# q's factors of units 10 and 11 contiguous, and another order of all engines, in a fused HGRN2 and leaky-ReLU MLP kernel

## The chip, the cores and the metric

One core of a Trainium2 chip runs the whole program. The metric is the device time of one execution in microseconds (us), as the median of several runs; a profile is taken of one further execution.

## The reference

A gated linear recurrence (HGRN2) over 768 steps feeds an MLP with a leaky ReLU. q, k, v and f_logit are [4, 8, 768, 48] (batch, heads, steps, head size), in float32.

```python
f = 1 / (1 + exp(-f_logit))
for t in range(S):
    state = f[:, :, t, :, None] * state + einsum('bhd,bhe->bhde', k[:, :, t], v[:, :, t])
    y[:, :, t] = einsum('bhd,bhde->bhe', q[:, :, t], state)
x = y.transpose(0, 2, 1, 3).reshape(3072, 384)
h = x @ w_in                      # w_in [384, 2048]
out = maximum(0.01 * h, h) @ w_out   # w_out [2048, 384]
```

## The kernel before

The recurrence is done in chunks of 128 steps, of which each batch has six. Work comes in twelve units `j`. Units 0 to 3 ("paired") hold one batch each, chunks 0 and 1 together. Units 4 to 11 ("unpaired") hold one chunk each of two batches: 4 and 5 are chunk 2 of batches 0, 1 and of 2, 3; 6 and 7 chunk 3; 8 and 9 chunk 4; 10 and 11 chunk 5, the last. `a` is 0 or 1 within a unit.

A unit runs so. Its f, k, q and v are loaded by SyncE's (SP's) queue (`Lf`, `Lk`, `Lq`, `Lv`, 192 KB each for one `a`, in pieces of 192 bytes for unpaired units). ScalarE (ACT) does the gate in two activations (`ge`, `gl`, lines L239 and L251); TensorE (PE) sums the log gates over steps (`cs`); ACT makes two sets of factors of the sums (`dec`), `em` for k (L306) and `at` for q (L308 or L311). VectorE (DVE) or GpSimd (POOL) multiply them into k and q (`k`, `q`, L322; L319 for the spread form). kh and qh are turned with the head size to the partitions: on PE for the paired units, and for the unpaired ones by two transposing DMAs in SP's queue (`xk`, `xq`, L363). PE then makes the scores (`sc`, L386), DVE masks them (`mk`, L400), PE mixes them with v and with the old state (`mx`, L417) and DVE or ACT copy the result to `xT` (`xt`). v is cast on DVE or POOL (`v`, L326). The state of a batch is carried on by `pt` (PE), `sf` (DVE) and `sb` (POOL, L510 and L513).

Then the MLP on PE: up-projections of 256 columns (`up`, L521) or, for the pairs of units 6, 7 and 8, 9, of 512 (`uw`, L532), the leaky ReLU on ACT (`pr`, L526, and `pv`, L535), and down-projections in four quarters (`dn`, L542; `dc`, L564, for half the columns of the last tile). `ob` copies a tile of the output from PSUM (L551, L553) to one of four buffers, and `st` stores it (L557). Weights are loaded (`WI`, `WO`) into the raw buffers of units 4 and 5 and cast (`ci`, `co`). `F` are matmuls on zeros whose results nobody reads.

`at` has two forms. Contiguous, it holds the 384 factors and behind them the factors at the chunk's end, which the state needs. Spread (`at_spread`), the factors stand so that two rows of 48 can be fetched by two small DMAs (`xe`, L295, 1.5 KB each) to a tile `end` on all the partitions that the state needs. Units 4 to 9 are in `SPREAD`; 10 and 11 have no state after them and need no `end`, but have the spread form too.

Every engine works in order and waits on semaphores. What stands in which place is written by hand in one string, `order`: each word is one operation of a unit, with the units and halves as numbers, the engine as a last number where there is a choice (0 DVE, 1 POOL or ACT, 2 both halves for loads of work that take a pair), and the PSUM banks behind `@`. The words are gone through from first to last, and each engine and SP's queue get theirs in that order; words of different engines beside each other say nothing of their times. Buffers are taken in turn: raw inputs by `j` mod 6, kh and qh by `j` mod 3, `at` by `j` mod 4, kT and qT by `j` mod 2, output buffers by `2j + a` mod 4.

Of the kernel before, what the change touches and what calls it, by code (L numbers as in the profile page):

```python
# [15 lines left out]
def kernel(  # L16
# [287 lines left out]
    def dec(j, a):  # L304
        t = banks[st[j]["cs", a]]
        nc.scalar.activation(ems[j % 2][:, a], t[:, 0:H * D], AF.Exp, scale=1.0)  # L306
        if spread(j):
            nc.scalar.activation(at_spread(j)[:, P2 * a:P2 * a + P2], t[:, 0:H * D].rearrange("t (p y d) -> t p y d", y=2, d=D),  # L308
                                 AF.Exp, scale=-1.0)
        else:  # L310
            nc.scalar.activation(at_of(j)[:, a], t[:, 0:H * D + P2], AF.Exp, scale=-1.0)  # L311
# [293 lines left out]
    tq_0_1@3 F_3_512@4 F_1_256@4 Lf_2_0 dec_1_1 k_1_1_1 tk_1_1@4 ge_2_1 gl_2_1 cs_2_1@2 Lq_1_0 WI_0 WI_1 sf_0_0
    sb_0_0 cq_0_1_1 ck_0_1_0 sc_0_1@5.7 F_1_512@3 F_1_256@3 ck_1_1_1 WI_5 q_1_1_1 tq_1_1@3 mk_0_0_0 sf_0_1
    Zk_2_0 mk_0_1_0 mk_0_0_1 Zb_1_0_1 sb_0_1 mk_0_1_1 WI_3 ge_1_0 gl_1_0 cs_1_0@0 v_1_1_1 cq_1_1_1 sc_1_1@6.4
    mk_1_1_1 mk_1_1_0 WI_2 dec_1_0 q_1_0_0 k_1_0_1 Lk_2_1 mx_0_2@5.1 ms_0 F_3_512@4 xt_0_1_0 dec_2_1 tq_1_0@3
    cq_1_0_0 ge_2_0 gl_2_0 Lq_2_1 xt_0_0_1 Lk_2_0 cs_2_0@7 dec_2_0 v_1_0_0 tk_1_0@0 F_2_512@3 F_1_256@3 ck_1_0_0
    sc_1_0@4.2 Lq_2_0 mk_1_0_1 Lv_2_1 pt_1_2@6.1 sf_1_0 ci_0_1 up_0_0@5 F_2_512@7 ci_1_1 up_0_1@3 ci_5_0  # L610
    up_0_5@0 mk_1_0_0 mx_1_2@7.2 xt_1_0_1 sb_1_0 sf_1_1 ms_1 Lv_2_0 ci_3_0 up_0_3@6 ci_2_0 up_0_2@4 xt_1_1_1
    up_1_2@1 up_1_1@7 k_2_1_1 tk_2_1@2 WI_4 WI_6 k_2_0_0 q_2_0_0 pr_0_0 up_1_5@5 pr_0_5 pr_0_2 ck_2_1_0 WO_0
    WO_1 pr_1_2 pr_0_1 q_2_1_1 tq_2_1@0 cq_2_1_0 tk_2_0@4 pr_1_5 Lf_3_1 WO_5 Lf_3_0 WO_3 ck_2_0_1 pr_0_3
    up_1_0@1 pr_1_0 tq_2_0@3 cq_2_0_0 v_2_0_0 up_1_3@2 pr_1_3 Mo WI_7 sc_2_0@5.0 mk_2_0_1 sc_2_1@4.6 mk_2_1_0
# [88 lines left out]
```

## Time and profile before

| | |
|---|---|
| median of 3 runs | 177.91 us (177.85 to 177.99) |
| the profiled execution's own time | 177.1 us |
| its span, from the first to the last instruction | 175.3 us |
| instructions | 5291 |
| HBM read and written | 25.17 MB and 4.72 MB, 170 GB/s over the span |
| granted TensorE clock | 1.000 |

A line of a group in the profile reads: source line, engine, operation, output<-input by the program's names, shape, count, then busy us and mean ns of one, then idle us of the engine just before. In a timeline, a row begins with start and length in us, and brackets at its end give the engine's idle time before it and what ended it. In a table by stretch, each row has the stretch, its length, then for PE, PE's weight loads, DVE, ACT and POOL the busy us and count, then the granted clock, the DMA share and GB/s. The DMA share is the busy share of the 16 DMA engines, and can pass 1 since packets overlap. SPq is SP's queue; its rows show how long the issue of a DMA held it.

### The profile page before, as it was taken

Reading aid. Unit: us, or ns where it says so; the run is one execution under the profiler, and the core shown is the slowest. Engines: PE = TensorE matmul, PEld = TensorE weight load, DVE = VectorE, ACT = ScalarE, POOL = GpSimd, SP = SyncE. Lnnn points to the kernel's source line nnn. Section 1 sums busy time; section 2 is a strip of 40 time slices with the busy share of each in tenths; the row PEclk is TensorE's granted clock in tenths of the full one; section 3 lists DMA queues with packets and bytes.
Section 4 is the critical chain, followed back from the end, with each engine's and each line's share of the span. In section 5 each row is a group of like instructions: output and inputs, shape, how many; then the busy total and the mean of one; then the engine's idle time right before and its main releaser. Section 6 shows DMA issues by size and latency. Waiting matters only on the chain.

```text
span 175.3 us, 5291 instructions
## 1 busy us (share of the span) xinstructions
PE 168.8 (96%) x2170; PEld 115.0 (66%) x2170; DVE 75.2 (43%) x159; ACT 110.2 (63%) x209; POOL 79.2 (45%) x131
## 2 busy tenths in 40 slices
...
DMA  5999988999995999999988899789989998411013
GB/s 155 323 313 354 287 232 271 384 265 293 228 227 126 224 196 233 148 191 196 175 172 193 184 175 222 163 163 188 226 171 237 187 209 174 105 40 45 0 59 124
DMA packets 109097, 34.45 MB, mean 197 GB/s; under 512 B 101776, under 2 KB 108048, under 8 KB 109072
## 3 DMA queue, kind: packets, MB, share of 16 engines
...
q8 instruction: 17, 0.28, 0.6%
...
HBM read 25.17 MB, written 4.72 MB: 170 GB/s over the span
## 4 chain that ended last, share of the span: by engine, by line
PE 45%; SPq 16%; DMA 11%; POOL 9%; DVE 8%; issue 5%; ACT 4%; POOLq 0%; DVEq 0%
PE ps L542 18%; PE ps L521 13%; SPq L212 9%; SPq L363 5%; PE ps L532 4%; DMA v_raw<-in_v_dram 4%; DMA k_raw<-in_k_dram 3%; DMA q_raw<-in_q_dram 2%; DMA out_dram<-osb 2%; PE ps L417 2%; DVE wm L400 2%; DVE wm L396 2%; SPq L295 2%; POOL kh L322 2%; PE ps L564 2%
## 5 line engine op out<-in xcount | busy, mean ns | idle before, releaser
L542 PE MATMUL ps<-w_out,gT 128*128 128x384 bf16 x368 | 66.6, 327 | 0.2 <-ACT gT L535 0.2
L542 PEld LDWEIGHTS <-gT 128*128 128x128 bf16 x368 | 34.9, 98 | 22.3 <-ACT gT L535 0.6
L526 ACT ACTIVATE gT<-ps 128x512 bf16<-128x512 f32 x64 | 34.8, 604 | 18.6 <-PE ps L521 18.2
L521 PE MATMUL ps<-xT,w_in 128*128 128x256 bf16 x384 | 45.6, 273 | 0.1
L521 PEld LDWEIGHTS <-w_in 128*128 128x128 bf16 x384 | 36.8, 98 | 6.4 <-DVE w_in L174 0.3
L400 DVE TENSOR_TENSOR wm<-ps,ut 128x512 bf16<-128x512 f32 x32 | 20.0, 684 | 25.3 <-PE ps L386 16.0
L322 POOL TENSOR_TENSOR kh<-k_raw,em 128x768 bf16<-128x768 f32 (+1 forms) x12 | 17.1, 1425 | 12.4 <-ACT em L306 5.9
L532 PE MATMUL ps<-xT,w_in 128*128 128x512 bf16 x96 | 22.1, 379 | 0.4 <-DVE osb L553 0.4
L535 ACT ACTIVATE gT<-ps 128x512 bf16<-128x512 f32 x32 | 17.7, 619 | 5.4 <-PE ps L532 5.1
L319 POOL TENSOR_TENSOR qh<-q_raw,at 128x768 bf16<-128x768 f32 x8 | 17.6, 2202 | 4.0 <-DMA q_raw<-in_q_dram 1.9
L513 POOL CAST sb<-sf 64x192 bf16<-64x192 f32 x40 | 14.9, 372 | 9.5 <-DVE sf L503 7.3
L553 DVE COPY osb<-ps 128x384 f32<-128x384 f32 x15 | 8.0, 553 | 24.2 <-PE ps L542 16.5
L306 ACT ACTIVATE em<-ps 128x384 bf16<-128x384 f32 x24 | 12.0, 500 | 8.8 <-PE ps L268 8.4
L475 ACT CAST xT<-ps 128x384 bf16<-128x384 f32 x15 | 7.2, 526 | 15.0 <-PE ps L417 15.0
L505 DVE TENSOR_TENSOR sf<-sf,ps 64x192 f32<-64x192 f32 x32 | 11.2, 350 | 12.3 <-PE ps L493 8.9
L532 PEld LDWEIGHTS <-w_in 128*128 128x128 bf16 x96 | 9.3, 98 | 10.9 <-issue 0.8
L510 POOL TENSOR_TENSOR sf<-sf,end 128x192 f32<-128x192 f32 x12 | 6.1, 506 | 20.8 <-DVE osb L553 11.0
L308 ACT ACTIVATE at<-ps 128x384 f32<-128x384 f32 x16 | 13.3, 831 | 0.0
L326 POOL CAST vb<-v_raw 128x384 bf16<-128x384 f32 (+1 forms) x9 | 6.1, 680 | 13.7 <-DMA v_raw<-in_v_dram 13.6
L239 ACT ACTIVATE f_raw<-f_raw 128x384 f32<-128x384 f32 (+1 forms) x16 | 11.0, 694 | 1.9 <-DMA f_raw<-in_f_logit_dram 1.9
L251 ACT ACTIVATE lf<-f_raw 128x384 bf16<-128x384 f32 (+1 forms) x16 | 11.0, 688 | 0.4
L396 DVE TENSOR_TENSOR wm<-ps,pair_mask 128x512 bf16<-128x512 f32 x16 | 10.4, 687 | 1.0 <-PE ps L379 0.8
...
## 6 DMA issues: line engine op xcount, KB each, us to landing
...
```

Of the source, the lines that this page charges most:

```text
L212: nc.sync.dma_start(out=raw(j, x)[:, a], in_=srcs[x][2 * h + a, :, c * C:(c + 1) * C, :].rearrange("h t d -> t h d"))
L308: nc.scalar.activation(at_spread(j)[:, P2 * a:P2 * a + P2], t[:, 0:H * D].rearrange("t (p y d) -> t p y d", y=2, d=D), AF.Exp, scale=-1.0)
L319: engine(e).tensor_mul(pairs(to[j % NR])[:, :, :, 0:D], pairs(raw(j, x)), at_spread(j))
L322: engine(e).tensor_mul(heads(j, to[j % NR], a)[:, :, :, 0:D], raw_heads(j, x, a), decays(j, by, a))
L396: nc.vector.tensor_mul(w.rearrange("t (s p) n -> t s p n", s=2), src.rearrange("t (s p n) -> t s p n", s=2, p=2), pair_mask[:, :, None, :] ...
L400: nc.vector.tensor_mul(w, src.rearrange("t (p n) -> t p n", p=P2), ut[:, None, :].to_broadcast([128, P2, 128]))
L513: nc.gpsimd.tensor_copy(out=sb[rows, :, y * D:y * D + D], in_=sf[rows])
L521: nc.tensor.matmul(pm[:, i, :], w_in_of(ff, kk), xT_of(j)[:, kk].rearrange("t a s -> t (a s)"), start=(kk == 0), stop=(kk == NK - 1))
L526: nc.scalar.activation(gT_of(j)[:, 2 * g:2 * g + 2, :], pm, AF.Prelu, alpha=0.01)
L532: nc.tensor.matmul(banks[bank], w_in_of(ff, kk), x[:, kk], start=(kk == 0), stop=(kk == NK - 1))
L535: nc.scalar.activation(gTs[n % 2][:, 512 * ff:512 * ff + 512], banks[st[2 * n].pop(("pw", ff))], AF.Prelu, alpha=0.01)
L542: nc.tensor.matmul(po, gT_of(j)[:, ff, 128 * a:128 * a + 128], w_out_b[ff // 2][:, ff % 2, :], start=(ff == 0), stop=(ff == NF - 1))
```

## The change

First, `spread(j)` is true for units 4 to 9 alone, so units 10 and 11 have the contiguous form, of 384 factors without those of the chunk's end. Their `q` product is then a plain product (L322) and no longer the spread one (L319).

Second, the whole `order` is another: the words are the same operations, but for the engine of some, the banks, one v load on ACT's queue in place of which a k load stands there now, and the zero matmuls, which are 22 of 512 and 4 of 256 columns before and 20 and 8 after.

```diff
     def spread(j):
-        return not paired(j) and (j in SPREAD or units[j][0] == NCH - 1)
+        return j in SPREAD
...
         else:
-            nc.scalar.activation(at_of(j)[:, a], t[:, 0:H * D + P2], AF.Exp, scale=-1.0)
+            n = H * D + P2 if paired(j) or chunk(j, a) < NCH - 1 else H * D
+            nc.scalar.activation(at_of(j)[:, a, 0:n], t[:, 0:n], AF.Exp, scale=-1.0)
...
     order = """
-    Zz Af_0_1 Av_0_0 F_9_512@7 Lf_0_0 Lf_1_1 Zl_1_1 Zk_0_0 Zb_2_0_1 Zv_2_1 Lk_0_0 Zv_0_0 Ms Lq_0_0 Mh Lv_0_1
+    Zz Af_0_1 Ak_0_1 F_9_512@7 Lf_0_0 Lk_0_0 Lf_1_1 Lq_0_0 Lq_0_1 Lv_0_1 Lv_0_0 Lf_1_0 Lk_1_1 Lq_1_1 Lv_1_1
...
```

Three places of the order. First SP's queue around the transposes of units 8 and 9 (kT0, qT0 are unit 8's, kT1, qT1 unit 9's; f_raw4 is f of unit 10, v_raw3 v of unit 9; `end` is written by the small transfers). Before:

```order
L212 DMA f_raw4_68<-in_f_logit_dram 128x8x48
L212 DMA q_raw3_79<-in_q_dram 128x8x48
L363 DMA_TRANSPOSE kT0_108<-kh2_93 128x8x128
L295 DMA end0_99<-at0_101 48x1x8
L363 DMA_TRANSPOSE qT0_110<-qh2_96 128x8x128
L295 DMA end1_100<-at1_102 48x1x8
L363 DMA_TRANSPOSE kT1_109<-kh0_91 128x8x128
L363 DMA_TRANSPOSE qT1_111<-qh0_94 128x8x128
L212 DMA v_raw3_85<-in_v_dram 128x8x48 x2
L295 DMA end1_100<-at1_102 48x1x8
L212 DMA f_raw5_69<-in_f_logit_dram 128x8x48
```

After:

```order
L558 DMA out_0_dram<-osb1_137 128x384
L364 DMA_TRANSPOSE kT0_108<-kh2_93 128x8x128
L364 DMA_TRANSPOSE qT0_110<-qh2_96 128x8x128
L558 DMA out_0_dram<-osb0_136 128x384
L364 DMA_TRANSPOSE kT1_109<-kh0_91 128x8x128
L364 DMA_TRANSPOSE qT1_111<-qh0_94 128x8x128
L212 DMA v_raw3_85<-in_v_dram 128x8x48 x2
L212 DMA f_raw4_68<-in_f_logit_dram 128x8x48
L212 DMA f_raw5_69<-in_f_logit_dram 128x8x48
L295 DMA end1_100<-at1_102 48x1x8
```

The two small transfers between the transposes are gone from there, a store stands in their place, and the second load of f for unit 10 moved from ahead of the four transposes to behind unit 9's v; 126 transfers of SP's queue stand ahead of it, where 117 did.

Second the same queue around the transposes of units 10 and 11 (kT0, qT0 and kT1, qT1; v_raw5 is v of unit 11). Before:

```order
L363 DMA_TRANSPOSE kT0_108<-kh1_92 128x8x128
L212 DMA k_raw5_75<-in_k_dram 128x8x48
L212 DMA q_raw5_81<-in_q_dram 128x8x48
L212 DMA k_raw5_75<-in_k_dram 128x8x48
L363 DMA_TRANSPOSE qT0_110<-qh1_95 128x8x128
L557 DMA out_0_dram<-osb0_136 128x384
L212 DMA v_raw5_87<-in_v_dram 128x8x48
L212 DMA v_raw4_86<-in_v_dram 128x8x48
L363 DMA_TRANSPOSE kT1_109<-kh2_93 128x8x128
L363 DMA_TRANSPOSE qT1_111<-qh2_96 128x8x128
L557 DMA out_0_dram<-osb1_137 128x384
L212 DMA v_raw5_87<-in_v_dram 128x8x48
```

After:

```order
L212 DMA k_raw5_75<-in_k_dram 128x8x48
L212 DMA v_raw4_86<-in_v_dram 128x8x48
L212 DMA q_raw5_81<-in_q_dram 128x8x48 x2
L212 DMA v_raw4_86<-in_v_dram 128x8x48
L558 DMA out_0_dram<-osb0_136 128x384
L364 DMA_TRANSPOSE kT0_108<-kh1_92 128x8x128
L364 DMA_TRANSPOSE qT0_110<-qh1_95 128x8x128
L558 DMA out_0_dram<-osb3_139 128x384
L364 DMA_TRANSPOSE kT1_109<-kh2_93 128x8x128
L364 DMA_TRANSPOSE qT1_111<-qh2_96 128x8x128
L558 DMA out_0_dram<-osb0_136 128x384
```

All loads now stand ahead of the four transposes, unit 11's second v among them.

Third, who makes kh and qh of units 10 and 11 (kh1, qh1 and kh2, qh2). Before, on POOL, its last rows:

```order
L322 TENSOR_TENSOR kh1_92<-k_raw4_74,em0_97 128x16x48
L319 TENSOR_TENSOR qh1_95<-q_raw4_80,at2_103 128x16x48
L510 TENSOR_TENSOR sf3_123<-sf3_123,end1_100 128x192
L513 CAST sb3_0_130<-sf3_123 64x4x48 x2
L510 TENSOR_TENSOR sf2_122<-sf2_122,end1_100 128x192
L513 CAST sb2_0_128<-sf2_122 64x4x48 x2
L510 TENSOR_TENSOR sf1_121<-sf1_121,end0_99 128x192
L513 CAST sb1_0_126<-sf1_121 64x4x48 x2
L322 TENSOR_TENSOR kh2_93<-k_raw5_75,em1_98 128x16x48
L319 TENSOR_TENSOR qh2_96<-q_raw5_81,at3_104 128x16x48
```

After, on DVE, for all but kh1, which stays on POOL:

```order
L323 TENSOR_TENSOR qh1_95<-q_raw4_80,at2_103 128x16x48
L554 COPY osb3_139<-ps6_146 128x384
L323 TENSOR_TENSOR kh2_93<-k_raw5_75,em1_98 128x16x48
L323 TENSOR_TENSOR qh2_96<-q_raw5_81,at3_104 128x16x48
L401 TENSOR_TENSOR wm1_113<-ps4_144,ut_154 128x512
```

The q products of units 5, 8 and 9 and the k products of units 6 and 9 went from POOL to DVE as well.

At other places that matter here: the first load of weights has 16 transfers of SP's queue ahead of it in both; the store for whose buffer the copy of unit 6's second tile waits stood behind unit 9's transposes and stands ahead of unit 8's; on ACT the gates of unit 10 stand ahead of the copy of unit 9's first half to `xT`; and the last up-projections of unit 11 before its first down chain are groups 2 and 3, which that chain's second quarter reads.

More of the change, by code (lines that the diff above doesn't have):

```diff
@@ L605 @@
[L605 to L614, printed above, removed]
@@ new lines @@
+    ck_1_1_1 cs_1_0@6 dec_1_0 q_1_0_0 tq_1_1@0 cq_1_1_1 mx_0_2@7.2 F_1_512@6 F_1_256@6 xt_0_0_0 Lq_2_1 WI_4
+    Lv_2_0 sb_0_0 ms_0 F_1_256@0 sf_0_1 tq_1_0@3 cq_1_0_0 Lv_2_1 v_1_1_1 sc_1_1@1.4 F_1_256@7 mk_1_1_0 mk_1_1_1
+    k_1_0_1 tk_1_0@6 v_1_0_1 ge_2_1 gl_2_1 cs_2_1@0 F_1_256@3 pt_1_2@7.5 sf_1_0 WI_6 ck_1_0_1 sc_1_0@3.6
+    F_1_512@1 mk_1_0_0 ci_0_1 WO_0 sb_1_0 ci_1_0 WO_1 ge_2_0 gl_2_0 cs_2_0@1 F_4_512@7 F_1_256@7 xt_0_1_1
+    up_0_0@4 F_1_512@3 pr_0_0 up_0_1@7 F_1_256@3 ci_5_0 up_0_5@2 sb_0_1 Lk_3_0 mk_1_0_1 mx_1_2@3.4 ms_1 Lf_3_0
@@ new lines @@
+    k_3_1_0 pr_0_7 dn_1_1_1 up_2_7@6 pr_2_7 dn_1_0_1 tk_3_1@2 co_5_0 Lk_5_0 Lk_5_1 dn_0_0_2 dn_1_0_2 dn_1_1_2
+    dn_0_1_2 dn_2_0_2 ck_3_1_1 ge_4_2 gl_4_2 cs_4_1@0 cs_4_0@6 dec_4_1 dec_4_0 xe_4_1 co_7_0 Lv_5_0 q_3_1_1
+    tq_3_1@2 co_6_1 Lq_5_0 Lq_5_1 dn_0_0_3 dn_1_1_3 dn_1_0_3 dn_0_1_3 ob_0_0_0 st_0_0 ob_1_1_1 st_1_1 ob_1_0_1
+    ob_0_1_1 st_0_1 cq_3_1_0 sc_3_1@0.3 v_4_2_1 sc_3_0@2.6 mk_3_0_1 mk_3_0_0 v_3_1_1 pt_3_2@1.7 dn_2_1_0@5
+    dn_2_1_1 dn_2_1_2 dn_2_1_3 sf_3_0 sb_3_0 ge_5_2 gl_5_2 cs_5_1@6 cs_5_0@2 dec_5_1 mk_3_1_0 mk_3_1_1
@@ new lines @@
+    mx_3_2@1.0 ms_3 xt_3_0_0 dn_2_0_3 k_4_2_1 xk_4 pt_4_0@3 pt_4_1@6 sf_4_0 sf_4_1 xt_3_1_1 up_3_5@1 up_3_4@0
+    up_3_2@3 up_3_0@6 pr_3_5 up_3_6@1 pr_3_4 up_3_3@0 dec_5_0 q_5_2_0 up_3_1@2 q_4_2_1 xq_4 pr_3_2 up_3_7@3
+    ob_2_0_0 pr_3_0 Lq_6_0 Lf_6_1 k_5_2_1 pr_3_1 dn_3_1_0@6 dn_3_0_0@4 pr_3_7 sf_3_1 sb_3_1 pr_3_3 dn_3_1_1
+    sc_4_2@2.7.3.0 mk_4_0_0 mk_4_1_0 mk_4_0_1 mk_4_1_1 dn_3_1_2 dn_3_0_1 dn_3_0_2 mx_4_2@2.3 xt_4_1_0 Lk_7_1
+    pr_3_6 dn_3_1_3 dn_3_0_3 Lf_6_0 ge_6_2 Lk_7_0 gl_6_2 cs_6_1@1 cs_6_0@7 dec_6_1 dec_6_0 Lv_5_1 xt_4_0_0
@@ new lines @@
+    dn_6_0_2 mx_8_2@1.7 xt_8_1_0 st_6_1 Lk_11_0 ge_10_2 gl_10_2 Lv_10_0 Lq_11_1 Lq_11_0 v_9_2_1 mx_9_2@3.2
+    xt_9_1_0 xt_9_0_1 Lv_10_1 dn_6_0_3 ob_6_0_1 st_6_0 sb_8_0 cs_10_0@0 dec_10_0 pt_9_1@5 sb_8_1 cs_10_1@7
+    dec_10_1 k_10_2_1 xk_10 pt_9_0@3 xt_8_0_0 uw_4_4@2 uw_4_13@1 uw_4_7@4 pv_4_7 uw_4_5@0 pv_4_5 uw_4_2@7 pv_4_2
+    uw_4_0@4 pv_4_0 uw_4_9@0 pv_4_9 pv_4_13 uw_4_8@7 pv_4_8 uw_4_14@4 uw_4_11@0 pv_4_11 uw_4_1@1 pv_4_14
+    uw_4_3@7 uw_4_15@0 uw_4_10@4 sf_9_0 uw_4_12@3 v_11_2_1 sf_9_1 uw_4_6@5 sb_9_1 pv_4_1 pv_4_3 dn_8_0_0@1
@@ new lines @@
+    dn_9_0_0@7 pv_4_4 dn_9_1_0@2 sb_9_0 q_10_2_0 xq_10 v_10_2_1 ob_7_1_0 dn_8_1_0@6 st_7_1 ge_11_2 gl_11_2
+    pv_4_12 cs_11_0@3 pv_4_6 cs_11_1@5 dn_8_0_1 dn_9_0_1 dn_8_1_1 dn_9_1_1 dec_11_1 pv_4_10 dn_9_0_2 dn_9_1_2
+    dn_8_0_2 dn_8_1_2 dec_11_0 k_11_2_0 xk_11 q_11_2_0 xq_11 pv_4_15 sc_10_2@5.4.3.0 mk_10_0_1 mk_10_1_0
+    mk_10_0_0 mk_10_1_1 dn_8_0_3 ob_8_0_1 dn_9_0_3 ob_9_0_0 dn_9_1_3 ob_9_1_1 mx_10_2@4.1 xt_10_0_0 xt_10_1_0
+    sc_11_2@3.5.0.2 mk_11_1_0 mk_11_0_0 mk_11_1_1 mk_11_0_1 dn_8_1_3 ob_8_1_0 up_10_0@7 up_10_1@4 pr_10_1
@@ L668 @@
+    dc_11_1_1_2 dc_11_1_0_0@4 dc_11_1_0_1 dc_11_1_1_3 oc_11_1_1_0 sh_11_1_1 dc_11_1_0_2 dc_11_1_0_3 oc_11_1_0_1
+    sh_11_1_0
     """
```

98 lines of the change are left out of this document (41 added, 57 removed).

## The prediction

> **What bounds the kernel now.** I read the page first (busy times, slices, chain), then busy time by stretch, then the timelines of PE, POOL and SP where the unpaired units run.
>
> ```profile
> PE 168.8 (96%) x2170; PEld 115.0 (66%) x2170; DVE 75.2 (43%) x159; ACT 110.2 (63%) x209; POOL 79.2 (45%) x131
> ...
> DMA  5999988999995999999988899789989998411013
> ...
> PE 45%; SPq 16%; DMA 11%; POOL 9%; DVE 8%; issue 5%; ACT 4%; POOLq 0%; DVEq 0%
> ```
>
> TensorE is busy for 96% of the span and looks like the only bound. But the 16 DMA engines are nearly as full until the 34th of the 40 slices, and the chain that ended last runs for 27% through SP's queue and through transfers. By stretch (the last two columns are DMA share and GB/s):
>
> ```profile
> 60.00:90.00 30.00, 30.00 (x361) 22.66 (x360) 10.70 (x22) 19.53 (x36) 15.40 (x14) 1.00 1.03 183
> 115.00:145.00 30.00, 29.04 (x305) 16.11 (x304) 10.10 (x20) 18.16 (x34) 15.30 (x19) 1.00 0.93 195
> ```
>
> So two queues run side by side, both full. At 195 GB/s one load of 192 KB takes 196,608 / 195e9 = 1.01 us. In the first stretch PE never waits; in the second it is idle for 0.96 us, in three waits of 0.17, 0.41 and 0.38:
>
> ```profile
> 117.23 1.15 PE L542 MATMUL ps<-w_out,gT 128*128 128x384 bf16 x6 [0.17 <-ACT gT L535]
> 121.56 0.62 PE L386 MATMUL ps<-qT,kT 48*128 48x128 bf16 x16 [0.41 <-DVE wm L400]
> ...
> 124.31 0.51 PE L417 MATMUL ps<-qT,sb 128*32 128x128 bf16 x24
> ...
> 129.81 4.05 PE L532 MATMUL ps<-xT,w_in 128*128 128x512 bf16 x18 [0.38 <-DVE osb L553]
> ...
> 148.99 0.62 PE L386 MATMUL ps<-qT,kT 48*128 48x128 bf16 x16
> ```
>
> ```profile
> 123.71 0.82 POOL L326 CAST vb<-v_raw 128x768 bf16<-128x768 f32 x1 [5.82 <-DMA v_raw<-in_v_dram]
> ...
> 143.58 2.19 POOL L319 TENSOR_TENSOR qh<-q_raw,at 128x768 bf16<-128x768 f32 x1
> ```
>
> POOL casts unit 9's v the moment it has landed, at 123.7 after 5.82 us of waiting, and PE mixes unit 9 at 124.31: the DMA queue sets PE's pace there. The last PE row is the scores of unit 11. What stands behind them on PE is the same set of operations in both kernels, so their start sets the end. SP's queue just ahead of such scores:
>
> ```profile
> 114.28 0.53 SPq L295 DMA_DIRECT2D end<-at  x1
> 114.91 1.25 SPq L363 DMA_TRANSPOSE qT<-qh  x1
> 116.26 0.53 SPq L295 DMA_DIRECT2D end<-at  x1
> 116.88 1.26 SPq L363 DMA_TRANSPOSE kT<-kh  x1
> 118.25 1.28 SPq L363 DMA_TRANSPOSE qT<-qh  x1
> ...
> 143.65 1.24 SPq L363 DMA_TRANSPOSE kT<-kh  x1
> 145.80 1.23 SPq L363 DMA_TRANSPOSE qT<-qh  x1
> ```
>
> ```profile
> qT<-qh SPq DMA_TRANSPOSE x8, 3.2
> ...
> end<-at SPq DMA_DIRECT2D x12, 1.5 KB, 2.4
> ```
>
> Unit 11's q transpose is issued at 145.80; with 3.2 us to landing that is 149.0, the start of the scores. POOL's product for it ends at 143.58 + 2.19 = 145.77, so SP stood from 144.89 to 145.80 for POOL: 0.91 us.
>
> **The change, part by part.**
>
> Zero matmuls. Before 22 of 512 columns and 4 of 256, after 20 and 8: two of 512 less and four of 256 more, the same columns. 0 us.
>
> q's factors of units 10 and 11. Four activations go from the spread to the contiguous form, whose nearest row is the paired units':
>
> ```profile
> L308 ACT ACTIVATE at<-ps 128x384 f32<-128x384 f32 x16 | 13.3, 831 | 0.0
> ...
> L311 ACT ACTIVATE at<-ps 128x388 f32<-128x388 f32 x8 | 4.1, 508 | 0.0
> ...
> L322 DVE TENSOR_TENSOR qh<-q_raw,at x5: 496/549/1205, 7.2 to 48.5; 128x384 bf16<-128x384 f32 x5
> ```
>
> 4 x (831 - 508) = 1.3 us of ACT. ACT is busy for 63% and PE waits for it 0.17 us in that stretch, so it counts 0; if this cover goes, the gain is up to 1.3.
>
> q's products. On POOL a spread one costs 2.2 us (the 2.19 above). After, those of units 5, 8, 9, 10 and 11 stand on DVE, and the k products of 6, 9 and 11 too. No row has such a DVE product of 768 columns: two of 384 at the median make 1.1 us, two of the longest 2.4. I take 1.1, for the median, with 2.4 for the range. Unit 11's two then take some 2.2 us on DVE, where POOL had to do state products first and took 1.6 + 2.2. SP's wait of 0.91 goes: -0.91. What is late next is the transfer queue itself.
>
> The end of SP's queue. Both v loads of unit 11 now stand ahead of the last four transposes; before, one of them stood behind. One load more ahead: +1.01.
>
> The small transfers of state factors (`end<-at`, 1.5 KB). Before, five of the twelve stand beside transposes or between them; after, one does, and the rest stand among loads and stores. The DMA share around these five, then around five that stand among loads (two of them in the window at 99.25):
>
> ```profile
> 75.50:76.50 1.00, 1.00 (x12) 0.90 (x10) 0.00 (x0) 1.00 (x3) 0.11 (x1) 1.00 0.25 35
> 83.75:84.25 0.50, 0.50 (x5) 0.29 (x4) 0.00 (x0) 0.50 (x2) 0.00 (x0) 1.00 0.45 83
> 92.50:93.50 1.00, 1.00 (x8) 0.61 (x7) 0.99 (x2) 1.00 (x2) 0.25 (x1) 1.00 0.23 41
> 115.50:116.25 0.75, 0.75 (x7) 0.43 (x6) 0.15 (x1) 0.72 (x2) 0.75 (x2) 1.00 0.22 38
> 117.50:118.25 0.75, 0.75 (x6) 0.29 (x4) 0.48 (x1) 0.00 (x0) 0.40 (x1) 1.00 0.20 36
> 96.25:97.25 1.00, 1.00 (x8) 0.61 (x7) 0.86 (x2) 0.00 (x0) 1.00 (x2) 1.00 0.29 66
> 99.25:99.75 0.50, 0.50 (x20) 0.46 (x12) 0.33 (x1) 0.50 (x3) 0.00 (x0) 1.00 0.46 114
> 123.00:123.50 0.50, 0.50 (x4) 0.14 (x2) 0.50 (x2) 0.00 (x0) 0.00 (x0) 1.00 0.43 59
> 129.25:130.00 0.75, 0.37 (x2) 0.10 (x1) 0.75 (x2) 0.54 (x1) 0.00 (x0) 1.00 0.26 46
> ```
>
> Lost time is the length times (1 - share). The first five: 0.75 + 0.28 + 0.77 + 0.59 + 0.60 = 2.99 us, 0.60 for each. The other four windows: 0.71 + 0.27 + 0.29 + 0.56 = 1.83, 0.37 for each of five transfers. Four that move save 4 x 0.23 = 0.9 us of the queue: -0.9, with bounds 0 (the transposes themselves make the holes) and -3.0 (all of the 2.99 goes). That some goes is likely from SP's rows: a transpose holds SP for 1.25 us, and the small transfer behind it for 0.53 more in which nothing large is issued.
>
> A rule of the Trainium skill speaks against this ("DMA: Bandwidth & Descriptors", Anatomy of one DMA): a transfer's fixed 2 us or so are mostly latency of completion and not setup, so a small one would hold nothing up behind it. The 2.4 us to landing of 1.5 KB agree with that figure. By the rule the moved transfers would save 0, and the sum would be 0.9 us higher.
>
> The queue's sum for unit 11's scores: 1.01 - 0.91 - 0.9 = -0.8 us.
>
> A second place, unit 10. Its second load of f stands behind unit 9's two v loads after, and stood ahead of unit 8's transposes before. Its gates on ACT:
>
> ```profile
> L239 ACT ACTIVATE f_raw<-f_raw 128x768 f32<-128x768 f32 x8 | 6.9, 861 | 0.0
> ...
> L251 ACT ACTIVATE lf<-f_raw 128x768 bf16<-128x768 f32 x8 | 6.8, 854 | 0.2
> ...
> 148.17 0.89 PE ps L417 x56
> ...
> 163.79 1.30 PE ps L542 x8
> ```
>
> It lands one load behind 123.7, at 124.7, less 0.9 at 123.8; with 0.86 + 0.85 and 0.1 of hand-over PE has its sums to do at 125.6. At the pace of before PE stands there at 124.31 + 0.89 for the mix + 0.65 for four down matmuls = 125.85. So PE may be 0.25 ahead there, and the 0.38 at 129.81 goes too, since unit 6's copy, for which it waits, hung on a store that is now issued ahead of unit 8's transposes: -0.6. Between -0.6 and -0.8 I take -0.7. The waits of 0.17 and 0.41 stand ahead of where the queue binds, so their going adds nothing.
>
> The start. PE's first up-projection stands at 18.55, and POOL casts its weights as they land:
>
> ```profile
> 16.33 0.82 POOL L174 CAST w_in<-f_raw 128x768 bf16<-128x768 f32 x1 [0.85 <-DMA f_raw<-in_moe_w_in_dram]
> ...
> 18.55 0.83 PE L521 MATMUL ps<-xT,w_in 128*128 128x256 bf16 x6
> ```
>
> As many transfers stand ahead of these weights after as before, so it comes up to 1.4 us earlier (18.55 - 17.15). I count 0, because PE gives back what it gains where the queue binds later. Bounds -1.4 and +0.5 (POOL's first products stand behind more clearing).
>
> The tail. The last two up groups of unit 11 now feed the second quarter of its first down chain, with one group of four down matmuls between them and it:
>
> ```profile
> L526 ACT ACTIVATE gT<-ps 128x512 bf16<-128x512 f32 x64 | 34.8, 604 | 18.6 <-PE ps L521 18.2
> ```
>
> Four down matmuls cover 0.65 us; the activation needs 0.60 and its two hand-overs some 0.2 to 0.3 (an estimate from the 0.17 above): +0.2, bounds 0 and 0.4.
>
> **Sum.** -0.7 + 0.2 = -0.5 us. The profiled execution took 177.1 us (a span of 175.3 and 1.8 around it), so 176.6. The median of the runs, 177.91, stands 0.8 above it: the forecast is 177.4.
>
> **Rivals.** 0.2% is 0.36 us, which I take for what can be told from no change.
>
> First, the queue gives nothing back, since the holes belong to the transposes, which remain. Then 1.01 - 0.91 + 0.2 = +0.3: 178.2, no change to be told. For it: the same bytes go through engines at a share of 0.93 to 1.03. Against it: the holes at 115.5 and 117.5, each beside a small transfer, are the deepest of all. By the page's rule above this is the outcome.
>
> Second, slower, by the late load of f for unit 10. PE stands at unit 10's sums for ACT's gates, and on ACT the copy that the wide up-projection of units 8 and 9 needs is queued behind them. It decides if that load lands after 124.0 (125.85 - 1.8). With no saving it lands at 124.7 and PE goes on at 126.5, 0.65 late; with 0.38 given back and 0.2 of tail that is +0.5, 178.4, and if one more load's time is lost in the queue, 179.4. For it: nine more transfers stand ahead of it than before. Against it: 0.7 us of saving is enough.
>
> Third, much faster: the 2.99 us of holes go, and the start keeps its gain. Then PE alone binds, its 0.96 us of waits end, and -1.4 - 0.96 + 0.2 = -2.2 gives 175.7. Against it: the queue would have to be ahead everywhere.
>
> **How the numbers follow.** The forecast has 0.45 and the third 0.1, both faster: 0.55. The first has 0.2: same. The second has 0.25: slower. The forecast's own range is 176.5 to 177.7 (a saving of 0.6 to 1.8); with the rivals' ends 175.9 to 178.5 leaves out 2 in 10.
>
> **What would show it.** Right: unit 11's scores start near 148.3; SP waits for no product ahead of the last q transpose; PE has no wait for `osb` in the wide up-projection of units 8 and 9; the DMA share between the transposes of units 8 and 9 is over 0.5. Wrong: PE idle ended by ACT's `lf` (L251) near 125 (the second rival); unit 11's scores at 149 or later with the transposes back to back (the first); DVE products of 768 columns at 2 us or more beside POOL's, which would put the 0.91 back.

## The result, and the profile after

The changed kernel took 178.81 us (median; 177.42 to 180.78) beside 177.81 us for the kernel before: a ratio of 1.0055, with a 95% interval of 1.003 to 1.008. It ran twice more, in other comparisons: 177.49 beside 177.59 us (1.0021, 0.9994 to 1.0049) and 177.39 beside 177.62 us (1.0014, 0.9988 to 1.004). So the change makes nothing faster; it costs nothing that can be told, or about half a per cent. The forecast of 177.4 us stood for a ratio of 0.997; that the repeats' times lie beside 177.4 is luck, since the kernel before took 177.6 there and not 177.91. The ratios count fast runs alone and are not the quotients of the medians, which are 0.9994 and 0.9987 in the repeats.

The time has two parts, the span from the first to the last instruction and what lies around it. In the repeats the median span is 175.4 and 175.2 us beside 175.8 for the kernel before, so 0.4 and 0.6 shorter (the means are 0.1 and 0.2 shorter). What lies around it is 2.08 to 2.26 us in all 44 runs of the changed kernel and 1.73 to 1.86 in all the runs of the kernel before that stand beside the experiments: medians of 2.12 to 2.15 and of 1.78. So what the repeats win inside the span, some 0.35 us outside it takes back.

The first execution profiled took 179.84 us, 1.0 above its median, with a span of 177.6 us. A second and a third took spans of 175.4 and 174.9. I show the first, and then what of it stood again. The busy line, the DMA share and the chain of its page:

```profile
PE 168.9 (95%) x2169; PEld 114.9 (65%) x2172; DVE 86.8 (49%) x170; ACT 110.8 (62%) x206; POOL 70.6 (40%) x123
...
DMA  5999999998994999996999988968896999120202
...
PE 59%; DMA 12%; POOL 8%; SPq 8%; issue 5%; DVE 4%; ACT 3%; POOLq 0%; ACTq 0%
```

TensorE's work is the same 169 us; DVE has 11.6 us more and POOL 8.6 less, as the products moved. PE's timeline, the rows with idle time in brackets and unit 11's scores:

```profile
91.94 0.62 PE L387 MATMUL ps<-qT,kT 48*128 48x128 bf16 x16 [0.62 <-ACT gT L527]
...
116.55 0.81 PE L533 MATMUL ps<-xT,w_in 128*128 128x512 bf16 x3 [0.90 <-DVE sf L506]
117.94 2.11 PE L543 MATMUL ps<-w_out,gT 128*128 128x384 bf16 x12 [0.58 <-DVE sf L506]
...
123.65 0.62 PE L387 MATMUL ps<-qT,kT 48*128 48x128 bf16 x16 [0.34 <-DMA qT<-qh]
...
151.22 0.62 PE L387 MATMUL ps<-qT,kT 48*128 48x128 bf16 x16
```

The waits of 0.41 and 0.38 that I had read before 130 us are replaced by others. The longest, 0.90, is for DVE's state sums of unit 8 (`sf`, L506), which free the PSUM bank of the next wide up-projection; 0.58 for the second of these sums follows at once. POOL, DVE and SP in that place:

```profile
113.74 1.57 POOL L511 TENSOR_TENSOR sf<-sf,end 128x192 f32<-128x192 f32 x1 [1.50 <-DMA end<-at]
```

```profile
113.46 1.47 DVE L320 TENSOR_TENSOR qh<-q_raw,at 128x768 bf16<-128x768 f32 x1 [3.69 <-DMA q_raw<-in_q_dram]
115.74 0.76 DVE L506 TENSOR_TENSOR sf<-sf,ps 64x192 f32<-64x192 f32 x2 [0.81 <-POOL sb L514]
117.13 0.76 DVE L506 TENSOR_TENSOR sf<-sf,ps 64x192 f32<-64x192 f32 x2 [0.63 <-POOL sb L514]
117.92 0.96 DVE L323 TENSOR_TENSOR kh<-k_raw,em 128x768 bf16<-128x768 f32 x1
118.80 1.45 DVE L320 TENSOR_TENSOR qh<-q_raw,at 128x768 bf16<-128x768 f32 x1
```

```profile
110.00 0.77 SPq L295 DMA_DIRECT2D end<-at  x1
...
115.00 1.23 SPq L364 DMA_TRANSPOSE qT<-qh  x1
116.28 0.57 SPq L558 DMA_DIRECT2D out_dram<-osb  x1
118.91 1.24 SPq L364 DMA_TRANSPOSE kT<-kh  x1
120.31 1.25 SPq L364 DMA_TRANSPOSE qT<-qh  x1
```

Read from the bottom up, this is a chain through four engines. SP has nothing to do from 116.85 to 118.91 (2.05 us): it waits for unit 9's k product on DVE. That product starts only at 117.92, behind two pairs of state sums. These wait for POOL's state products of unit 6, and the first of those waits until 113.74 for a transfer of 1.5 KB that SP issued at 110.00. Before, the last of unit 9's transposes was issued at 118.25; here at 120.31.

I call this the state chain. The second profile has it too, without the wait for the transfer:

```profile
111.59 1.61 POOL L511 TENSOR_TENSOR sf<-sf,end 128x192 f32<-128x192 f32 x1
...
113.64 0.76 DVE L506 TENSOR_TENSOR sf<-sf,ps 64x192 f32<-64x192 f32 x2 [0.81 <-POOL sb L514]
...
113.26 1.43 SPq L364 DMA_TRANSPOSE qT<-qh  x1
114.74 0.57 SPq L558 DMA_DIRECT2D out_dram<-osb  x1
116.81 1.24 SPq L364 DMA_TRANSPOSE kT<-kh  x1
118.22 1.25 SPq L364 DMA_TRANSPOSE qT<-qh  x1
```

Here unit 8's q transpose is issued 1.65 us earlier than before (113.26 for 114.91), so the order does gain on the queue there; then SP waits 1.50 us for unit 9's k product, and the last transpose is issued at 118.22, where it was before (118.25). The gain is spent in one wait. In the third profile these are 112.49, a wait of 1.97, and 117.81; in the first, where unit 8's q transpose went out at 115.00, there was no gain to spend.

### The profile page after: what moved, and what is told of

Its sections match the earlier page's. It is cut to its first block, busy times and chain, and to the rows that moved or that the text cites. A ratio compares the mean times of both kernels' runs of the same rounds, so it can differ in the third digit from the quotient of the medians.

```text
span 177.6 us, 5295 instructions
## 1 busy us (share of the span) xinstructions
PE 168.9 (95%) x2169; PEld 114.9 (65%) x2172; DVE 86.8 (49%) x170; ACT 110.8 (62%) x206; POOL 70.6 (40%) x123
## 4 chain that ended last, share of the span: by engine, by line
PE 59%; DMA 12%; POOL 8%; SPq 8%; issue 5%; DVE 4%; ACT 3%; POOLq 0%; ACTq 0%
PE ps L543 22%; PE ps L522 18%; SPq L212 5%; PE ps L418 4%; DMA v_raw<-in_v_dram 4%; DMA qT<-qh 4%; PE ps L533 4%; POOL qh L320 2%; DMA end<-at 2%; POOL sf L511 2%; POOL sb L514 2%; DMA f_raw<-in_f_logit_dram 2%; PE ps L387 2%; SPq L558 2%; PE ps L565 1%
## 5 line engine op out<-in xcount | busy, mean ns | idle before, releaser
L543 PE MATMUL ps<-w_out,gT 128*128 128x384 bf16 x368 | 65.3, 326 | 0.7 <-DVE sf L506 0.6
L527 ACT ACTIVATE gT<-ps 128x512 bf16<-128x512 f32 x64 | 36.1, 605 | 19.1 <-PE ps L522 14.7
L536 ACT ACTIVATE gT<-ps 128x512 bf16<-128x512 f32 x32 | 18.1, 604 | 5.0 <-PE ps L533 4.4
L514 POOL CAST sb<-sf 64x192 bf16<-64x192 f32 x40 | 16.3, 408 | 11.9 <-DVE sf L504 9.4
L327 POOL CAST vb<-v_raw 128x768 bf16<-128x768 f32 (+1 forms) x13 | 9.5, 738 | 18.7 <-DMA v_raw<-in_v_dram 18.4
L554 DVE COPY osb<-ps 128x384 f32<-128x384 f32 x12 | 6.6, 553 | 20.4 <-PE ps L543 10.9
L511 POOL TENSOR_TENSOR sf<-sf,end 128x192 f32<-128x192 f32 x12 | 7.1, 593 | 21.0 <-DVE osb L554 10.5
L323 POOL TENSOR_TENSOR kh<-k_raw,em 128x768 bf16<-128x768 f32 (+1 forms) x9 | 11.9, 1318 | 8.5 <-ACT gT L536 5.5
L552 ACT COPY osb<-ps 128x384 f32<-128x384 f32 x11 | 5.1, 491 | 13.3 <-PE ps L543 13.2
L506 DVE TENSOR_TENSOR sf<-sf,ps 64x192 f32<-64x192 f32 x32 | 11.2, 350 | 3.8 <-POOL sb L514 1.4
L323 DVE TENSOR_TENSOR kh<-k_raw,em 128x384 bf16<-128x384 f32 (+1 forms) x7 | 5.6, 807 | 11.0 <-ACT em L306 10.9
L100 PE MATMUL ps<-zeros 128*128 128x512 bf16 (+1 forms) x28 | 9.3, 430 | 1.2 <-DVE zeros L93 1.1
```

Source lines behind the costliest of these rows:

```text
L323: engine(e).tensor_mul(heads(j, to[j % NR], a)[:, :, :, 0:D], raw_heads(j, x, a), decays(j, by, a))
L506: nc.vector.tensor_add(sf[rows], sf[rows], new)
L514: nc.gpsimd.tensor_copy(out=sb[rows, :, y * D:y * D + D], in_=sf[rows])
L527: nc.scalar.activation(gT_of(j)[:, 2 * g:2 * g + 2, :], pm, AF.Prelu, alpha=0.01)
L536: nc.scalar.activation(gTs[n % 2][:, 512 * ff:512 * ff + 512], banks[st[2 * n].pop(("pw", ff))], AF.Prelu, alpha=0.01)
L543: nc.tensor.matmul(po, gT_of(j)[:, ff, 128 * a:128 * a + 128], w_out_b[ff // 2][:, ff % 2, :], start=(ff == 0), stop=(ff == NF - 1))
```

## The experiments

The theory: the order gains on the transfer queue, and SP gives it back in waits for products that stand on DVE behind work that is itself late (unit 9's behind the state sums, unit 6's k product behind two state sums and a copy). The rivals: the transfers set the pace whatever their order; or the loss lies in the opening, in the layout, or in the last units. In each, the ratio is to the kernel before on the same chip. In the cuts of the order, a plus marks a word put in and a minus one taken out.

**after_again.** No edit.

> The changed kernel once more, beside the others of this call. Its first profile was of an execution of 179.84 us, 1.0 above the median of 178.81, so that its waits may overstate what the change costs. Theory of the state chain (the 0.90 us that TensorE waits near 116.5 for DVE's state sums of unit 8, and SP's wait of 2.05 us for unit 9's k product behind them, belong to the order): both waits stand in this profile again, within 0.5 us. Rival (they were chance of one execution: a small transfer that happened to take 3.7 us to land): they are gone or under 0.3 us, at the same median of 178.8. A third place, the wait of 0.62 us ahead of unit 6's scores, is asked in the same way.

177.49 us, 1.0021 (0.9994 to 1.0049). The 0.62 at 92 us was gone, the 0.90 and 0.58 shrank to one wait of 0.29, and SP's wait to 1.50:

```profile
115.85 2.11 PE L543 MATMUL ps<-w_out,gT 128*128 128x384 bf16 x12 [0.29 <-DVE sf L506]
...
121.58 0.62 PE L387 MATMUL ps<-qT,kT 48*128 48x128 bf16 x16 [0.36 <-DMA qT<-qh]
```

This is between the two expectations. SP's wait for unit 9's k product belongs to the order: it stood in all three profiles, and with it a wait of 0.34 to 0.36 of TensorE for unit 9's q transpose. TensorE's waits for the state sums do not stand: they fell under 0.3 here, which was the rival's mark, and were gone in the third profile. The half per cent of the first comparison does not come back.

**end_early.** Three small transfers earlier, in one row.

```
  xe_7_0 +xe_7_1 +xe_6_1 +xe_6_0 Lf_9_1 Lv_8_1 Lq_9_0 Lk_8_0 ...
  ... -xe_7_1 sb_7_1 sb_7_0 Lq_9_1 -xe_6_1 ... q_8_2_0 -xe_6_0 sb_6_0 sf_8_0 sb_6_1 sf_8_1
```

> The changed kernel, with three small transfers of state factors (both halves of unit 6, the second of unit 7) moved up SP's queue to stand behind the first of unit 7, near 97.9 us, in place of 106.1, 107.3 and 110.0. No other queue changes. Theory of the state chain: POOL then has its state products of units 6 and 7 done by about 109, DVE's state sums of unit 8 wait for no one, TensorE's 0.90 us near 116.5 and SP's 2.05 us go, unit 9's scores start some 1 to 2 us earlier against the work ahead of them: about 177.8, 1.0 below the changed kernel. Rival (the whole transfer queue is late, and the next load takes the place of what goes): 178.6 to 178.9. Second rival (three more small transfers ahead of the loads cost the 0.4 to 0.6 us each that I had read from the holes in the DMA share): unit 8's products are 1 to 2 us later, 178.8 to 179.5.

177.31 us, 0.9986 (0.9963 to 1.0008); the changed kernel itself took 177.49 beside it, so the 1.0 us expected did not come. SP's wait for unit 9's k product was gone (0.17 us), yet unit 9's q transpose was issued at 118.25 again. The row of four small transfers took its price ahead of it:

```profile
96.00:98.00 2.00, 2.00 (x53) 1.41 (x54) 2.00 (x5) 1.10 (x3) 0.94 (x2) 1.00 0.93 230
98.00:100.00 2.00, 2.00 (x97) 1.64 (x86) 1.62 (x5) 1.48 (x3) 0.07 (x1) 1.00 0.08 11
100.00:102.00 2.00, 1.95 (x16) 1.10 (x16) 1.84 (x6) 0.20 (x1) 0.00 (x0) 1.00 0.72 137
```

By stretch, with the DMA share next to last: SP issued the four from 96.18 to 98.63, and for two microseconds the DMA engines then had almost nothing. That is 1.84 + 0.56 = 2.4 us of the queue. Without the row, in the second profile of the changed kernel, the last two stretches had shares of 0.93 and 0.77, so the three transfers that moved cost 1.70 + 0.10 = 1.8 us more, 0.6 for each.

**before_opening.** The kernel before up to about 21 us, the changed order behind.

```
  the first 158 steps of the order before, then the changed order's steps without those done
```

> The order of the kernel before up to about 21 us (the first 158 steps), and from there the changed kernel's order without the steps already done (six steps differ, two PSUM banks are renamed). The layout is the changed one. In the profiles TensorE's first up-projection stood at 18.55 before and at 19.19 after. Theory of the opening (0.64 us are lost there, and TensorE is too full afterwards to win them back): about 178.2, 0.6 below the changed kernel. Rival (what is lost there would be spent again in waits for the transfer queue at 92 and at 116): 178.7 to 178.9, with longer waits at these places.

178.12 us, 1.005 (1.0026 to 1.0075). TensorE's first up-projection stood at 18.50, but unit 2's mix at 32.20 (32.15 in the changed kernel, 32.00 before): all but 0.15 of the 0.64 us of the opening are given back within 14 us. So the opening is not where the time goes. That the time is near the 178.2 expected is luck: it is above the 177.49 of the changed kernel beside it, and was to be below. The state chain stood, with an SP wait of 2.03 and 1.08 of TensorE's for unit 9's q transpose; why this one was 0.3 per cent above after_again I can't say.

**layout_alone.** The kernel before with the contiguous layout for units 10 and 11.

```
-        return not paired(j) and (j in SPREAD or units[j][0] == NCH - 1)
+        return j in SPREAD
...
```

> The kernel before with the new layout alone: q's factors of units 10 and 11 contiguous, order and engines as before, so that these products stay on POOL. In the changed kernel's profile POOL's product of 768 columns took 2.20 us in the spread form and 1.64 in the contiguous one. Theory of the queue (SP waits 0.91 us for POOL's product ahead of unit 11's q transpose, and that transpose sets the end): POOL ends its two products 1.1 us earlier, SP's wait goes, and the time falls by 0.4 to 0.6 to about 177.3. Rival (TensorE gets to unit 11's scores late anyway, and SP's waits cost nothing): 177.8, no change to be told.

177.13 us, 0.9983 (0.9957 to 1.001): no change to be told, though the median fell as the first theory has it. SP's wait ahead of unit 11's q transpose shrank from 0.91 to 0.52. Unit 11's scores in this profile:

```profile
144.57 1.23 SPq L364 DMA_TRANSPOSE qT<-qh  x1
```

```profile
148.56 0.62 PE L387 MATMUL ps<-qT,kT 48*128 48x128 bf16 x16
```

The transpose is issued 1.23 us sooner than before (144.57 for 145.80), and the scores start 0.43 sooner, without a wait in either kernel.

**both_waits.** The small transfers earlier one by one, and unit 6's k product one state sum earlier.

```
  sf_5_0 +xt_5_0_0 +k_6_2_0 sf_5_1 ... -xt_5_0_0 ... -k_6_2_0
  Lv_8_1 +xe_7_1 Lq_9_0 Lk_8_0 +xe_6_1 ... Lk_9_1 +xe_6_0 Lf_9_0 ... -xe_7_1 ... -xe_6_1 ... -xe_6_0
```

> The changed kernel with the two waits of SP's queue for DVE's products taken on at once: unit 6's k product stands one state sum earlier on DVE (in both profiles of the changed kernel it began at 85.58, and SP stood 1.78 us for it in the second), and the three small transfers of units 6 and 7 go up SP's queue again, this time one by one among the loads between 98 and 104 us and not in one row (in the kernel with all of them in one row SP's wait of 1.50 to 2.05 for unit 9's k product was gone, but the DMA share fell to 0.81 around them and unit 9's q transpose was issued at 118.25 as before). Theory of the products (SP's waits for DVE take away what the order gains on the queue): both waits fall under 0.5 us, unit 9's q transpose is issued near 117.0, and the time is 176.7 to 177.1, 0.3 to 0.5 per cent below the kernel before. Rival (the transfers themselves set the pace up to unit 9's v, whatever their order): the transpose is issued at 118 again and the time is that of the kernel before, 177.4 to 177.7.

176.29 us, 0.9945 (0.9916 to 0.9974): faster than both kernels. Its busy line, chain, two PE groups, and the same places on POOL, DVE and SP:

```profile
PE 168.5 (97%) x2172; PEld 115.3 (66%) x2172; DVE 87.2 (50%) x170; ACT 111.1 (64%) x206; POOL 69.4 (40%) x123
...
PE 88%; DVE 4%; DMA 2%; issue 2%; ACT 2%; POOL 1%; POOLq 0%; ACTq 0%
...
L543 PE MATMUL ps<-w_out,gT 128*128 128x384 bf16 x368 | 65.3, 326 | 0.1
L533 PE MATMUL ps<-xT,w_in 128*128 128x512 bf16 x96 | 21.4, 379 | 0.0
```

```profile
107.55 0.51 POOL L511 TENSOR_TENSOR sf<-sf,end 128x192 f32<-128x192 f32 x1
...
112.72 1.49 DVE L506 TENSOR_TENSOR sf<-sf,ps 64x192 f32<-64x192 f32 x4
114.24 0.96 DVE L323 TENSOR_TENSOR kh<-k_raw,em 128x768 bf16<-128x768 f32 x1
...
115.23 1.36 SPq L364 DMA_TRANSPOSE kT<-kh  x1
116.69 1.25 SPq L364 DMA_TRANSPOSE qT<-qh  x1
```

POOL has unit 6's state product done 4 us sooner, DVE's sums run without a wait, SP stands 0.51 us, and the last transpose is issued at 116.69, 1.5 us sooner than in the other two. TensorE has no wait of 0.15 us or more behind 60 us, and the chain that ended last is now TensorE for 88%, where it was 59% (45% before). The time is below the 176.7 that was the least expected.

**before_end_moved.** Tests my term for the small transfers on the kernel before.

```
  xk_8 -xe_8_0 q_8_2_1 xq_8 ... -xe_9_1 k_9_2_1 xk_9 q_9_2_1 xq_9 ... Lv_9_0 Lv_9_1 +xe_8_0 +xe_9_1 xe_9_0
```

> The kernel before with one edit: the two small transfers of state factors that stand between the four transposes of units 8 and 9 are moved behind unit 9's v loads. My prediction took from the DMA share that such a transfer costs the queue 0.60 us beside a transpose and 0.37 among loads, and SP issues each for 0.53. By that the last of the four transposes is issued 1.1 us earlier (117.1 for 118.25), the wait of 0.41 ahead of unit 9's scores goes, and the time falls by 0.3 to 0.5 to about 177.2. Rival (the holes belong to the transposes, or SP would have stood there for POOL's products anyway): issued at 117.9 or later, 177.6, no change.

179.16 us, 1.0084 (1.0052 to 1.0116): slower, which neither expectation had. SP and POOL at the transposes:

```profile
113.72 1.23 SPq L363 DMA_TRANSPOSE qT<-qh  x1
117.10 1.23 SPq L363 DMA_TRANSPOSE kT<-kh  x1
119.25 1.23 SPq L363 DMA_TRANSPOSE qT<-qh  x1
...
115.43 1.65 POOL L322 TENSOR_TENSOR kh<-k_raw,em 128x768 bf16<-128x768 f32 x1 [0.47 <-POOL sb L513]
```

and, from the windows:

```profile
116.00:118.00 2.00, 2.00 (x16) 1.22 (x14) 0.70 (x2) 1.97 (x5) 2.00 (x2) 1.00 0.11 22
...
124.00:126.00 2.00, 2.00 (x108) 1.62 (x110) 1.57 (x3) 0.44 (x2) 0.82 (x1) 1.00 0.08 12
```

The hole between the transposes stays and deepens (0.11), because SP waits there 2.16 us for POOL's k product. This execution was late as a whole by then: that product began 1.34 us after its time before (114.09). TensorE had waited 0.75 and 0.48 us for weights near 23 us, far ahead of the edit; the profile of last_part, with the same opening, has two like waits there (0.80 and 0.48). Taken from there, the last transpose, at 119.25 for 118.25, is 0.34 us earlier, not 1.1: the small transfers had stood mostly in waits. The three in a row then make a second hole (0.08 from 124 to 126), the stores behind them are late with it, and TensorE waits for an output copy, where it had waited 0.38:

```profile
132.15 4.04 PE L532 MATMUL ps<-xT,w_in 128*128 128x512 bf16 x18 [1.71 <-DVE osb L553]
```

The chain that ended last runs through these small transfers, a store behind them and this copy. So of the 2.7 us by which this span is longer, 1.33 hang on where the transfers went; some 1.2 were lost ahead of the edit.

**first_half** and **last_part.** Half of each order.

```
  first_half: the first 515 steps of the changed order, then the rest of the order before
  last_part:  the first 639 steps of the order before, then the rest of the changed order
```

> The changed order up to unit 5's down-projection near 92 us (its first 515 steps), and the order of the kernel before from there (eight steps differ, three PSUM banks are renamed), with the old layout for units 10 and 11. Theory of the margin (the changed order has unit 6's transposes land 0.3 us ahead of its scores where before they had some 2, and unit 9's product behind the state sums on DVE; only the first of these is in this kernel): 177.6 to 178.0. Rival (all that is lost is lost in the first half): 178.3 or more. Second rival (all that is lost is lost behind 92 us): 177.4 to 177.6.

> The order of the kernel before up to unit 10's gates near 116 us (its first 639 steps), and the changed order from there, with the changed layout (seven steps differ, 14 PSUM banks are renamed). It has the changed kernel's loads, products on DVE and last down chain of units 10 and 11, and none of its waits for unit 6's and unit 9's products. Theory of the products: nothing is lost here, 177.2 to 177.5. Rival (the late load of f for unit 10, or the last down chain with its 0.2 us, loses by itself): 177.9 or more, with TensorE waiting for ACT's gates of unit 10 near 126 or at the last down chain.

184.15 us (1.0396) and 180.14 us (1.0151). Both are inconclusive: the seams themselves stall TensorE, which waits for output copies that neither whole order has late:

```profile
94.80 4.05 PE L542 MATMUL ps<-w_out,gT 128*128 128x384 bf16 x16 [3.11 <-DVE osb L553]
```

```profile
124.03 0.62 PE L387 MATMUL ps<-qT,kT 48*128 48x128 bf16 x16 [1.32 <-ACT osb L552]
```

Two finished orders can't be cut and joined where they are this tight.

**end_late.** The dose the other way.

```
  q_8_2_0 +Lf_10_1 +Lk_9_0 +st_4_1 +xk_8 xe_6_0 sb_6_0 sf_8_0 sb_6_1 sf_8_1 ... -Lf_10_1 -Lk_9_0 -st_4_1 -xk_8
```

> The dose the other way: the changed kernel with one small transfer later, unit 6's first half behind unit 8's k transpose instead of ahead of a load of f, one of k and a store. Theory of the state chain: POOL's state product of unit 6, which began at 111.6 in the second profile of the changed kernel, begins at 115 to 116 when this transfer has landed; DVE's state sums of unit 8 and unit 9's products, which stand behind them in DVE's order, move by 2.5 to 3.5 us with it, SP waits 3.5 to 5 us for the k product, unit 9's scores are 2 to 3 us later, and the time is 1.5 to 3 us above the changed kernel of this work (177.5 to 178.8): 179.5 to 181. Rival (the products' place in DVE's order is of no matter, the loads set unit 9): 178 at most.

180.96 us, 1.0187 (1.0155 to 1.022), within the theory's range and far from the rival's. Its rows:

```profile
116.27 0.50 POOL L511 TENSOR_TENSOR sf<-sf,end 128x192 f32<-128x192 f32 x1 [4.24 <-DMA end<-at]
...
117.21 0.76 DVE L506 TENSOR_TENSOR sf<-sf,ps 64x192 f32<-64x192 f32 x2 [3.53 <-POOL sb L514]
...
120.38 1.24 SPq L364 DMA_TRANSPOSE kT<-kh  x1
...
118.02 1.44 PE L533 MATMUL ps<-xT,w_in 128*128 128x512 bf16 x3 [3.13 <-DVE sf L506]
```

One transfer of 1.5 KB, issued at 113.43 instead of 108.84, moves POOL, DVE, SP and TensorE by 3 to 5 us each and the time by 3 us.

**k6_alone** and **ends_spread.** The two halves of both_waits.

> The changed kernel with the first half of the kernel that took on both waits: unit 6's k product one state sum earlier on DVE, the small transfers left where the changed kernel has them. Theory: it gives unit 6's k transpose 1 us of margin, which counts only in executions with slow transfers (0.62 us of TensorE at unit 6's scores in one profile, nothing in the other), so 0 to 0.3 us: 177.4 to 178.2, unit 9's transposes still at 118 and TensorE still idle near 116 and 121. Rival (this was the part that paid): 176.3 to 176.9.

> The other half: the three small transfers of units 6 and 7 one by one among the loads between 98 and 104 us, unit 6's k product left in its place. Theory of the state chain: this is the part that paid, POOL's state products are done by 110, SP's wait for unit 9's k product is under 0.6 us, its q transpose is issued near 117, and the time is 176.2 to 176.9. Rival (the gain was unit 6's product, or needs both): 177.3 or more.

177.25 us, 0.9979 (0.9954 to 1.0003), and 176.83 us, 0.9964 (0.994 to 0.9987). k6_alone is a little below the least expected, 177.4. The small transfers by themselves make the kernel faster than the kernel before: SP's q transpose of unit 9 went out at 117.08, as against 118.50 with k6_alone. The other half can't be told from nothing against the kernel before. Both start from the changed kernel, though, whose repeats stand at 1.0021 and 1.0014, and the two intervals overlap; so it isn't shown that one half pays more than the other, nor what unit 6's product adds to the transfers.

**both_old_layout.** both_waits with the spread layout of units 10 and 11.

> The kernel with both waits taken on (176.29 us, ratio 0.9945 to the kernel before), and q's factors of units 10 and 11 back in the spread form, so that the layout is the only difference to that kernel. In the profiles DVE's q product of 768 columns took 1.45 us in the spread form and 0.96 contiguous, and ACT's factor 0.83 and 0.51. Theory of cover (ACT and DVE are idle beside these products, and the transposes of units 10 and 11 land ahead of TensorE): 176.2 to 176.5, no difference. Rival (unit 11's transposes go 0.5 to 1 us later by the longer products and TensorE waits for them): 176.8 to 177.3.

176.16 us, 0.9932 (0.9907 to 0.9957): no difference to both_waits. DVE's last q product took 2.07 us here (1.09 in the changed kernel) and TensorE did not wait for it.

**after_third** and **both_waits_again.** Repeats on one chip.

> The changed kernel a third time, on the same chip as the kernel before and the one with both waits taken on. Theory of the thin margin (the change itself costs 0.2 to 0.5 per cent, and more in executions whose transfers are slow, since unit 6's transposes and unit 8's state sums come just in time): ratio 1.001 to 1.006, with a wider spread than both_waits has. Rival (no effect at all, the first comparison was chance): 0.998 to 1.001.

> The kernel with both waits taken on once more. Theory of the products: 0.9945 again, 0.992 to 0.997, and its times within 1 us of each other but for one or two. Rival (half of its gain was chance): 0.998 or more.

1.0014 (0.9988 to 1.004), times from 177.09 to 180.56; and 0.9943 (0.9916 to 0.997), times from 176.11 to 177.49. The gain of both_waits stood again, and the changed kernel again can't be told from the kernel before. Its spread was the wider one here (3.5 us beside 1.4), as the theory of the thin margin has it, but in the earlier comparisons it was 1.9 beside 1.7, so the runs don't settle that.

## Why the prediction was wrong

Two steps failed. One is the queue's sum for unit 11, 1.01 - 0.91 - 0.9: TensorE did not wait for the queue at the place that the sum was worked out for, and within the sum the small transfers and the products were priced wrong. The other is a term put at nothing, the time around the span.

- **Unit 11's scores as the place that counts: not so, in the kernel before either.** That 145.80 + 3.2 comes out at the start of the scores was taken to mean that the transpose sets it. But their row, 148.99, has no bracket, and the last one ahead of it is the 0.38 at 129.81. The chain that ended last, before, runs on TensorE alone from there to its last matmul:

```profile
129.20 0.57 DVE osb L553
129.81 4.05 PE ps L532 x18
...
149.06 0.55 PE ps L386 x16
```

layout_alone took the transpose 1.23 us forward, and the scores started without a wait as before. What TensorE had to win between 115 and 145 us was its own 0.96 us of waits. both_waits, which has none there, starts these scores at 147.99, 1.00 sooner than before.
- **Around the span, 1.8 in both: wrong.** It is 2.12 to 2.15 in the changed kernel (medians), some 0.35 us that stood nowhere in the sum. They go with the order and not with the layout (1.76 in layout_alone, 2.17 in both_old_layout), and neither half of the order has them alone (1.79 in first_half and in last_part); end_early, with three words moved, has 1.92. What they consist of stays open.
- **Small transfers, -0.9: did not come.** Behind the holes at 115.5 and 117.5 SP would have waited for POOL's products anyway; before_end_moved took the two small transfers away, and its transposes gained 0.34 us. Nor are these holes the deepest of all: one as deep and twice as long stood where SP issued loads and a store alone, 3 us ahead of the next small transfer:

```profile
109.75:111.25 1.50, 1.50 (x9) 0.77 (x8) 0.35 (x1) 1.50 (x4) 1.42 (x2) 1.00 0.20 32
```

I had put the price at 0.60 beside transposes and 0.37 among loads. The runs show 0.6 for each in a row of four, and little for one that stands in a wait. The Trainium skill ("DMA: Bandwidth & Descriptors", Anatomy of one DMA) has a transfer's fixed time as mostly latency of completion, in a section on transfers issued from GpSimd; those here are issued from SP. The cheap ones agree with it, the share of 0.08 behind a row of four does not. I also failed to count all that stands ahead of unit 9's q transpose: two small transfers and a load of f leave, and two stores of 192 KB come.
- **Products to DVE, -0.91: half right.** The size was right for q in the contiguous form, by the rows below: 1.03 us on average against my 1.1. In the spread form of units 5, 8 and 9 it is 1.74, within my 2.4. And SP waits no more ahead of unit 11's q transpose. But I priced how long a product lasts and not what stands ahead of it on DVE. The wait came back as 1.50 to 2.05 us at unit 9, and at unit 6 as 1.78 in the second profile and 1.89 in the third. Of these last, 1.1 to 1.2 us are the product's own: beside POOL's k product it took 2.08 and 2.13 us, where it had 0.96 in the first profile, which was a sign of being wrong that the prediction named. "What is late next is the transfer queue itself" was the false sentence.

```profile
L320 DVE TENSOR_TENSOR qh<-q_raw,at 128x768 bf16<-128x768 f32 x3 | 5.2, 1740 | 5.4 <-DMA q_raw<-in_q_dram 3.7 <-ACT at L308 1.7
...
L323 DVE TENSOR_TENSOR qh<-q_raw,at 128x768 bf16<-128x768 f32 x2 | 2.0, 1025 | 5.0 <-DMA q_raw<-in_q_dram 5.0
```

- **Unit 10, -0.6: did not come as a whole.** TensorE's wait of 0.38 for `osb` went, in all three profiles; the 0.25 by which it was to be ahead did not come. The f load could be no earlier than the transposes ahead of it. Unit 9's mix stood at 124.33 in the second profile and 124.31 before, and TensorE then passed the gates. The second rival's wait for `lf` is real but small: 0.36 us in end_early, 0.15 in after_third, none in the first profile.
- **One load more, +1.01: not on the path.** Unit 11's scores began without a wait in all three profiles of the changed kernel (151.22, 148.99, 148.56). TensorE set them, not the queue.
- **Zero matmuls and ACT's factors, 0: right.** Both layouts gave the same time in both_old_layout and both_waits.
- **The start, 0: right in its effect**: it was 0.64 late, just past my bound of 0.5, and all but 0.15 was made up for by 32 us. **The tail, +0.2: not there**; no PE wait of 0.15 us stands behind 126 us in any of the three.

Of the rivals, the first (the queue gives nothing back, no change) came nearest in the two repeats, but its reason, holes that belong to the transposes, isn't what the runs show. The first comparison, 178.81, lies above my range and in that of the second rival (178.4 to 179.4), but by luck: TensorE waited for no `lf` near 125 in the execution profiled there. That execution started unit 11's scores 2.23 us later than the second; 0.62 of it are the wait ahead of unit 6's scores, and 1.19 the state chain's waits of TensorE (0.90 + 0.58 against 0.29). At unit 6, TensorE's weight load waited 0.90 us for the k transpose, and in the state chain POOL waited 1.50 us for a small transfer. In the one stretch compared its transfers were slower (169 GB/s between 60 and 70 us, 186 and 177 in the other two profiles). That slow transfers cost more in this order, because unit 6's transposes and unit 8's state sums come just in time, is argued and not shown; why they were slower stays open, and with it whether the change by itself costs 0.2 per cent or nothing.
